# Attention and two MLPs on one core: six half buffers of values for four, block 0's sums allocated later, another order of loads

## The chip, the cores and the metric

The kernel runs on one core of a Trainium2 chip. The metric is the device time of one execution in microseconds (us), the median over several runs. Profiles come from one further execution taken with the hardware profiler; their times count from the span's start.

## The reference

The reference computes attention for 4 batches (blocks below) of 8 heads, with 32 global and 512 local rows of 64 numbers, and sends all 2304 rows of 512 numbers through two MLPs. A local row sees the 32 global keys and the local keys within a distance of 32; a global row sees all 544 keys.

```
mask = np.abs(pos[:, None] - pos[None, :]) <= window      # window = 32
out_g = matmul(softmax(scale * q_g @ k_all^T), v_all)
out_l = matmul(softmax([scale * q_l @ k_g^T, masked scale * q_l @ k_l^T]), [v_g, v_l])
x = concat(out_g, out_l) -> (2304, 512)
h = x @ w_in;  g = where(h > 0, h, exp(min(h, 0)) - 1);  x = g @ w_out        # 512 -> 2048 -> 512
h = x @ w_in2; g = where(h >= 1, h, where(h <= -1, 0, (h + 1)**2 / 4)); y = g @ w_out2
```

## The kernel before

**Two stages.** Lines 634 to 750 are attention, written in a fixed order: every instruction goes through `Pinned` (lines 103 to 111), which keeps each engine's program order, and shows as L111 in the profile. Lines 754 to 820 are the two MLPs; from `eng = free` (line 751) on, the framework's scheduler orders the instructions. Numbers of 32 bits are split into a high and a low part (`xh`, `xl`, `gh`, `gl`, `wh`, `wl`), so that each product is made of three matmuls.

**Attention in slots.** Two heads are a pair: pairs 0 to 15, four to a block. `units` (line 634) holds 24 units in threes: the local rows of an even pair 2g, the global rows of pairs 2g and 2g+1, the local rows of the odd pair 2g+1. The loop at line 719 runs slots n = 0 to 25. In slot n the engines do: scores of unit n (TensorE, tiles `s` or `sg`), division by the sums for unit n-2 (VectorE, `den`, `o_sb`, `og`), transposes of unit n-1 (TensorE `pt` or `tg`, copied by ScalarE to `pT` or `pgT`), transposes of unit n-2 (`ot` or `tg3`, which the trace names `tg`), its high and low part (`xh`, `xl`), the maximum and exponential of unit n (`sn`, `nml`), one step of the weights' preparation, one or two steps of the first five MLP tiles (`early_ups`, from slot 9 on), and the product of unit n-1 with the values (`po` or `pog`). A triple of slots below is slots 3g to 3g+2; s(n) means the scores of slot n.

**What each unit needs.** Scores of a local unit read queries `q_sb` and spread keys `kw`, which GpSimd builds from `k_sb` (`spread_keys`, four instructions for a pair, two for each half). Scores of a global unit read `k_sb` and `diag`, which GpSimd fills from the queries of both its pairs (`spread_queries`). The product with values reads `v_sb`, two half buffers a pair; the global unit reads both halves of both its pairs. There are two buffers each of `q_sb` and `k_sb`, four of `kw` and four half buffers of values (`load_v`, line 415, `bufs=4`).

**Loads.** `load` (line 124) issues on SyncE's queue, in program order. Each load counts the 4-byte words that it brings a partition: 544 for queries, 576 for keys, 1040 for half of a pair's values, 1024 for a part of the weights. From the seventh load on it waits until so many of its elders have landed that at most 2700 words are under way (`IN_FLIGHT`). It also waits, in the queue, until the last reader of its buffer is done. `arrive(n)` (line 700) runs at each slot's end. In slot 3g (g > 0) it sends the odd pair's first half of values, in slot 3g+1 the queries and keys of pair 2g+2 and the odd pair's second half, in slot 3g+2 the queries and keys of pair 2g+3 and both halves of pair 2g+2.

**Weights.** Three tiles of the first MLP's weights are prepared during attention, as six parts of 512 columns. They share one buffer `wraw`. A part is sent at the end of slots 1, 3, 6, 9, 12 and 15 (line 744). Its three steps (lines 178 to 198: VectorE `rest`, then `top`, then `power` and `wl`) run one a slot from slot `PREP_AT = 2` on; the second step is the last reader of `wraw`.

**Storage.** `acc0`, block 0's sums (8 KB a partition), is allocated in `xpool` (line 371) before attention, although its first write comes in slot 24. The tile `e` (2 KB, line 255) of the second MLP's curve is in `t_p`, also open throughout. `zeros` (1 KB, line 642) feeds the ten warm-up matmuls `idle`.

Of the kernel before, what the change touches and what calls it, by code (L numbers as in the profile page):

```python
# [9 lines left out]
F32 = mybir.dt.float32  # L10
BF16 = mybir.dt.bfloat16
# [9 lines left out]
B, H, SL, SG, D = 4, 8, 512, 32, 64  # L21
# [4 lines left out]
P = 128  # L26
NPAIR = H // 2
NSUB = SL // 32
VW = D + 1
KPAD = S + 32  # L30
KT = DM // P
# [15 lines left out]

BANKS = (2, 3, 1)

PREP_AT = 2  # L50
UP_AT = 9

UP_STEP = 4
# [11 lines left out]
def band_attention_then_two_mlps(  # L65
# [21 lines left out]
    xpool = ctx.enter_context(tc.tile_pool(name="x", bufs=1))  # L87
    t_p = ctx.enter_context(tc.tile_pool(name="tmp", bufs=2))
    h_p = ctx.enter_context(tc.tile_pool(name="h", bufs=LAG + 2))
    ps_up = [ctx.enter_context(tc.tile_pool(name="ps_up", bufs=1, space=PSUM))]  # L90
    ps_dn = []

    mask_sb = const.tile([P, 3, P], F32, name="mask_sb")
    eye_sb = const.tile([P, P], F32, name="eye_sb")
# [6 lines left out]
    acc = {}  # L101
# [17 lines left out]
    eng = pinned  # L119
# [4 lines left out]
    def load(out, src, words):  # L124

        ins = eng.sync.dma_start(out, src)
        if eng is not pinned:
            return
        flying, older = words, len(loads)
        while older and flying + loads[older - 1][1] <= IN_FLIGHT:  # L130
            older -= 1
            flying += loads[older][1]
        if older and len(loads) >= FIRST_LOADS:
            tc.add_manual_dep(
                ins.ins, loads[older - 1][0].ins.name, LANDED, reason="loads in flight"
            )
        loads.append((ins, words))
# [6 lines left out]
    for layer in range(2):  # L144
        f = 0
# [4 lines left out]
    def add_ring(pool, i):  # L150

        n = max(len(fs) for _, fs in chunks[i::2])
        ring[i] = [pool.tile([P, n, WCOLS], F32R, name=f"w{nm}{i}") for nm in "hl"]
# [62 lines left out]
    class Up:  # L216
# [31 lines left out]
        def curve(self):  # L248
            self.g = t_p.tile([P, SL], F32, tag="g", name="g")[:, :self.n]
            if self.layer == 0:  # L250
                eng.scalar.activation(self.g, self.ps, AF.Exp)  # L251

                eng.scalar.activation(self.g, self.g, AF.Relu, bias=one_sb, scale=-1.0)  # L253
            else:
                self.e = t_p.tile([P, SL], F32, tag="e", name="e", bufs=1)[:, :self.n]
                eng.scalar.activation(self.g, self.ps, AF.Relu, bias=half_sb, scale=0.5)  # L256
                eng.scalar.activation(self.e, self.ps, AF.Relu, bias=nhalf_sb, scale=0.5)  # L257

# [108 lines left out]
    def mpool(name, bufs, **kw):  # L367
        return ctx.enter_context(tc.tile_pool(name=name, bufs=bufs, reuse_waits="tile", **kw))

    add_ring(ctx.enter_context(tc.tile_pool(name="w", bufs=1)), 0)  # L370
    acc[0] = xpool.tile([P, KT, SL], F32, name="acc0")
    prep_ctx = ExitStack()
    wtmp_p = prep_ctx.enter_context(tc.tile_pool(name="wtmp", bufs=1))

    with ExitStack() as actx:
        def apool(name, bufs, **kw):
            return actx.enter_context(tc.tile_pool(name=name, bufs=bufs, **kw))
# [3 lines left out]
        st_p = apool("st", 4, side="right")  # L381
        sp_p = apool("sp", 4, side="right")
        raw_p = apool("raw", 2, side="right")
        win_p = apool("win", 4, side="right")
        g_p = apool("gl", 1, side="right")
# [4 lines left out]
            tc.tile_pool(name="ps_s", bufs=BANKS[0], space=PSUM, side="right")  # L390
        )

        diag = [g_p.tile([P, 64], F32, name=f"diag{i}") for i in range(4)]

        def normalised(po, out):

# [3 lines left out]
            eng.vector.reciprocal(den, den)  # L400
            eng.vector.tensor_tensor(out, po[..., 0:D], den.to_broadcast([P, *n, D]), ALU.mult)

        loaded = {}
        half = NSUB // 2

        def load_qk(b, hp):
            q_sb = raw_p.tile([P, S], F32, tag="q", name="q_sb")
            k_sb = raw_p.tile([P, KPAD], F32, tag="k", name="k_sb")
            both = [(q_sb, qT), (k_sb, kT)]
            for sb, dram in both if b + hp else both[::-1]:  # L410
                load(sb, dram[b, hp], sb.shape[1])
            loaded[b, hp] = [q_sb, k_sb, diag[(NPAIR * b + hp) % 4], [], []]

        def load_v(b, hp, es=(0, 1)):
            for e in es:
                v_sb = win_p.tile([P, half, 2, VW], F32, tag="v", name="v_sb", bufs=4)
                load(v_sb, vwin[b, hp, :, half * e:half * e + half], half * 2 * VW)
                loaded[b, hp][4].append(v_sb)

        def spread_keys(b, hp):  # L420

            k_sb, kws = loaded[b, hp][1], loaded[b, hp][3]
            for e in range(2):
                kw = win_p.tile([P, half, P], F32, tag="kw", name="kw")
                band = bass.AP(
                    tensor=k_sb.tensor,
                    offset=k_sb.offset + SL // 2 * e,
                    ap=[k_sb.ap[0], [32, half], [1, 96]],
                )
                glob = bass.AP(  # L430
                    tensor=k_sb.tensor, offset=k_sb.offset, ap=[k_sb.ap[0], [0, half], [1, 32]]
                )
                if b + hp + e == 0:
                    eng.vector.tensor_copy(kw[:, :, 0:96], band)
                    eng.scalar.activation(kw[:, :, 96:P], glob, AF.Copy)
                else:
                    eng.gpsimd.tensor_scalar(kw[:, :, 0:96], band, 1.0, 1.0, ALU.mult, ALU.mult)
                    eng.gpsimd.tensor_scalar(kw[:, :, 96:P], glob, 1.0, 1.0, ALU.mult, ALU.mult)
                kws.append(kw)

        def spread_queries(b, hp):

            for c in (hp - 1, hp):
                if hp % 2:
                    q_sb, dq = loaded[b, c][0], loaded[b, c][2]
                    for h in range(2):
                        r = 64 * h
                        eng.gpsimd.tensor_scalar(
                            dq[r:r + 64, 32 * h:32 * h + 32], q_sb[r:r + 64, 0:32], 1.0, 1.0,
                            ALU.mult, ALU.mult,  # L450
                        )
# [186 lines left out]
        pairs = [(b, hp) for b in range(B) for hp in range(NPAIR)]  # L638

        halves = [(f, c0, WCOLS // 2) for c0 in (0, WCOLS // 2) for f in range(W_EARLY)]  # L640

        zeros = st_p.tile([P, 512], BF16, name="zeros", bufs=1)
        eng.vector.memset(zeros, 0.0)
        eng.vector.memset(half_sb, 0.5)
        eng.scalar.activation(st_p.tile([P, 1], F32, name="unused", bufs=1), half_sb, AF.Exp)
        idle = ps_s.tile([P, 512], F32, tag="s", name="idle")
# [4 lines left out]
        eng.scalar.dma_start(eye_sb, eye)  # L651
        load_qk(*pairs[1])
        load_v(*pairs[0])
        for t in diag:
            eng.vector.memset(t, 0.0)
        eng.vector.memset(nhalf_sb, -0.5)
        eng.vector.memset(one_sb, 1.0)
        spread_keys(*pairs[0])
# [6 lines left out]
        def early_weights():  # L665

            for part in parts:
                for _ in range(3):
                    next(part, None)
                    yield  # L670
# [19 lines left out]
        sent = iter(parts)  # L690
        weights, ups = early_weights(), early_ups()
# [8 lines left out]
        def arrive(n):  # L700

            g, r = divmod(n, 3)
            more = 2 * g + 2 < len(pairs)
            if r == 0 and 2 * g + 1 < len(pairs):
                if g:
                    load_v(*pairs[2 * g + 1], es=(0,))
                    spread_queries(*pairs[2 * g + 1])
            elif r == 1 and 2 * g + 1 < len(pairs):
                if more:
                    load_qk(*pairs[2 * g + 2])  # L710
                load_v(*pairs[2 * g + 1], es=(1,) if g else (0, 1))
                spread_keys(*pairs[2 * g + 1])
            elif r == 2 and more:
                load_qk(*pairs[2 * g + 3])
                load_v(*pairs[2 * g + 2])
                spread_keys(*pairs[2 * g + 2])

        live, first = {}, {}
        for n in range(len(units) + 2):
            if n > UP_AT:  # L720
                next(ups, None)
            part(n, "scores")
            part(n - 2, "norm")
            part(n - 1, "turn")
            part(n - 1, "copy")
            part(n - 2, "back")
            part(n - 2, "high")
            part(n, "top")
            part(n - 2, "low")
            part(n, "expo")  # L730
            if n >= PREP_AT:
                next(weights, None)
            if n >= UP_AT:
                next(ups, None)
            part(n - 1, "values")

            arrive(n)
            if n == len(units):

                s_ctx.close()  # L740
                ps_dn.append(mpool("ps_dn0", 1, space=PSUM))
                for f in chunks[0][1]:
                    down(0, chunks[0][1], 0, f, made[0, f, 0], first, range(KT // 2))
            if n == 1 or n % 3 == 0 < n:
                next(next(sent, iter([0])))
        for _ in weights:
            pass
        for _ in ups:
            pass
        prep_ctx.close()  # L750
        eng = free


# [1 line left out]
    for j in range(1, B):  # L755
        acc[j] = pool.tile([P, KT, SL], F32, name=f"acc{j}")
    acc[GR] = pool.tile([P, KT * P], F32, name="acc_rows")
    wraw_p = mpool("wraw", 1, side="right")
    wtmp_p = mpool("wtmp", 1, side="right")
    add_ring(mpool("w_more", 1, side="right"), 1)  # L760
# [124 lines left out]
```

## Time and profile before

| | |
|---|---|
| median of 3 runs | 871.76 us |
| lowest, highest | 871.65, 876.94 us |
| the profiled execution's own time | 871.46 us |
| its span, first to last instruction | 869.7 us |
| TensorE busy | 851.4 us, 98% of the span |
| VectorE, ScalarE, GpSimd busy | 584.3, 432.7, 47.6 us |
| moved by DMA | 65.43 MB |

The profiled execution took 1.76 us more than its span, and lies 0.30 us under the median. Its page divides the span into 40 slices of 21.7 us; the first six are attention. In rows of the time order, the number after a bracket is the idle time of the engine just before the row, and the name behind the arrow is what ended it.

### The profile page before, as it was taken

To read this page: it belongs to the slowest core of one execution; us is meant where nothing else is said; L and a number is where in the kernel's file an instruction comes from. 1 tells how busy PE (TensorE), PEld (TensorE's weight loads), DVE (VectorE), ACT (ScalarE), POOL (GpSimd) and SP (SyncE) were. 2 spreads that over 40 slices of the span, in tenths; PEclk is the share of its full clock that TensorE was granted. 3 is DMA by queue.
4 is the path that set the end of the run, shared out by engine and by line. 5 is a ranking of instruction groups with operands and counts; after the bars stand their busy time and mean duration, and the time that the engine had idled before them with its cause. 6 is when DMAs were issued, how large, how long until landed. Compare 5 with 4: busy or idle time off the path is not lost.

```text
span 869.7 us, 14553 instructions
## 1 busy us (share of the span) xinstructions
PE 851.4 (98%) x5946; PEld 697.9 (80%) x5946; DVE 584.3 (67%) x1130; ACT 432.7 (50%) x755; POOL 47.6 (5%) x98
## 2 busy tenths in 40 slices
PE   7889999999999999999999999999999999999998
PEld 5667778888888888888888888888888888888886
DVE  4769874877636873833389897368859754845455
ACT  5758774766434543534257564456435433433332
POOL 4324320000000000000000000000000000000000
PEclk9989999999999999999999999999999999999999
DMA  7767751231200220110012112002201200000014
GB/s 258 246 220 246 235 176 58 104 131 52 94 1 1 96 97 1 49 48 1 1 49 96 49 50 97 0 4 97 95 0 49 97 1 1 0 1 1 2 58 148
DMA packets 19027, 65.43 MB, mean 75 GB/s; under 512 B 3984, under 2 KB 4240, under 8 KB 15248
## 3 DMA queue, kind: packets, MB, share of 16 engines
q1 hardware_dynamic: 18672, 64.23, 21.3%
q8 instruction: 47, 0.77, 0.3%
q10 hardware_dynamic: 288, 0.26, 0.1%
q14 instruction: 20, 0.16, 0.1%
HBM read 60.03 MB, written 4.46 MB: 74 GB/s over the span
## 4 chain that ended last, share of the span: by engine, by line
PE 91%; DMA 5%; DVE 2%; ACT 1%; issue 0%; SPq 0%
PE dn L318 40%; PE up L245 39%; DMA v_sb<-in_vwin 3%; PE up L242 3%; PE dn L335 3%; DMA wraw<-in_w 2%; PE up L111 1%; PE pt L111 1%; PE s L111 1%; PE po L111 1%; PE pog L111 1%; PE sg L111 1%; PE dn L111 0%; PE tg L111 0%; DVE rest L111 0%; DVE top L111 0%
## 5 line engine op out<-in xcount | busy, mean ns | idle before, releaser
L318 PE MATMUL dn<-gh,wh 128*128 128x512 f32 x506 | 196.9, 389 | 0.0
L318 PE MATMUL dn<-gl,wh 128*128 128x512 f32 x506 | 196.8, 389 | 0.0
L318 PE MATMUL dn<-gh,wl 128*128 128x512 f32 x506 | 196.3, 390 | 0.0
L245 PE MATMUL up<-xh,wl 128*128 128x512 f32 x492 | 192.4, 391 | 0.0
L245 PE MATMUL up<-xl,wh 128*128 128x512 f32 x492 | 191.6, 390 | 0.0
L245 PE MATMUL up<-xh,wh 128*128 128x512 f32 x492 | 191.6, 389 | 0.0
L276 ACT ACTIVATE gh<-g 128x512 fp32r<-128x512 f32 x123 | 77.8, 632 | 118.7 <-DVE g L265 71.9
L295 DVE TENSOR_TENSOR acc<-dn,acc 128x512 f32<-128x512 f32 x128 | 84.9, 686 | 48.5 <-PE dn L318 48.4
L280 DVE TENSOR_TENSOR gl<-g,gh 128x512 fp32r<-128x512 f32 x123 | 84.7, 689 | 39.1 <-ACT gh L276 38.1
L318 PEld LDWEIGHTS dn<-gl,wh 128*128 128x128 f32 x506 | 95.0, 188 | 19.9
L318 PEld LDWEIGHTS dn<-gh,wh 128*128 128x128 f32 x506 | 95.0, 188 | 19.5
L318 PEld LDWEIGHTS dn<-gh,wl 128*128 128x128 f32 x506 | 95.0, 188 | 19.3
L245 PEld LDWEIGHTS up<-xh,wh 128*128 128x128 f32 x492 | 92.3, 188 | 19.3
L245 PEld LDWEIGHTS up<-xl,wh 128*128 128x128 f32 x492 | 92.4, 188 | 18.8
L245 PEld LDWEIGHTS up<-xh,wl 128*128 128x128 f32 x492 | 92.4, 188 | 18.7
L256 ACT ACTIVATE g<-up,half_sb 128x512 f32<-128x512 f32 (+1 forms) x69 | 47.0, 680 | 113.5 <-PE up L245 104.7
L264 DVE SCALAR_TENSOR_TENSOR g<-g 128x512 f32<-128x512 f32 (+1 forms) x69 | 46.9, 680 | 59.4 <-ACT g L256 59.4
L262 DVE SCALAR_TENSOR_TENSOR g<-up,g 128x512 f32<-128x512 f32 x64 | 43.5, 679 | 62.9 <-ACT g L253 62.9
L251 ACT ACTIVATE g<-up 128x512 f32<-128x512 f32 x64 | 37.8, 591 | 87.5 <-PE up L245 82.1
L265 DVE TENSOR_TENSOR g<-g,e 128x512 f32<-128x512 f32 (+1 forms) x69 | 47.0, 681 | 3.6
L178 ACT ACTIVATE top<-wraw 128x1024 f32<-128x1024 f32 x29 | 33.6, 1160 | 27.8 <-DMA wraw<-in_w 24.0
L257 ACT ACTIVATE e<-up,nhalf_sb 128x512 f32<-128x512 f32 (+1 forms) x69 | 46.6, 676 | 0.3 <-DVE g L265 0.3
(112 smaller groups left out, 955.1 us busy)
## 6 DMA issues: line engine op xcount, KB each, us to landing
wraw<-in_w SPq DMA_DIRECT2D x29, 1024.0 KB, 4.8
v_sb<-in_vwin SPq DMA_DIRECT2D x32, 520.0 KB, 4.5
k_sb<-in_kT SPq DMA_DIRECT2D x16, 288.0 KB, 3.8
q_sb<-in_qT SPq DMA_DIRECT2D x16, 272.0 KB, 4.2
outT<-acc SPq DMA_DIRECT2D x16, 256.0 KB, 2.1
wraw<-in_w SPq DMA_DIRECT2D x6, 512.0 KB, 4.7
outT<-acc_rows SPq DMA_DIRECT2D x4, 64.0 KB, 2.2
mask_sb<-in_mask ACTq DMA_DIRECT2D x1, 192.0 KB, 3.3
```

Of the source, the lines that this page charges most:

```text
L111: return lambda *args, **kw: tc.keep_in_program_order(fn(*args, **kw))
L245: eng.tensor.matmul(self.ps, w, x, start=k == 0, stop=k == 3 * KT - 1)
L251: eng.scalar.activation(self.g, self.ps, AF.Exp)
L256: eng.scalar.activation(self.g, self.ps, AF.Relu, bias=half_sb, scale=0.5)
L257: eng.scalar.activation(self.e, self.ps, AF.Relu, bias=nhalf_sb, scale=0.5)
L262: eng.vector.scalar_tensor_tensor(g, self.ps, 0.0, g, ALU.max, ALU.subtract)
L264: eng.vector.scalar_tensor_tensor(g, g, 1.0, g, ALU.min, ALU.mult)
L265: eng.vector.tensor_tensor(g, g, self.e, ALU.add)
L276: eng.scalar.activation(self.gh, self.g, AF.Copy)
L280: eng.vector.tensor_tensor(self.gl, self.g, self.gh.bitcast(F32), ALU.subtract)
L295: eng.vector.tensor_tensor(a, ps, a, ALU.add)
L318: eng.tensor.matmul(banks[d], w[:, d * P:(d + 1) * P], g, start=f == fs[0] and k == 0, stop=f == fs[-1] and k == 2,)
```

## The change

Six half buffers of values stand in place of four. The room comes from `acc0`, now allocated at slot 24 after the preparation's scratch pool is closed, from `e`, allocated after attention in a pool of its own, and from `zeros`, now the same storage as the four `diag` tiles (one memset for both).

`arrive` sends in another order. In slot 0 the values of pair 1; in slot 1 the queries and keys, then the values, of pair 2; in slot 3g (g > 0) both halves of pair 2g+2; in slot 3g+1 its queries and keys; in slot 3g+2 the queries and keys of pair 2g+3, then a part of the weights, then both halves of pair 2g+3. So the parts of the weights are sent in slots 2, 5, 8, 11, 14 and 17, and are prepared from slot 4 on. GpSimd spreads the even pair's keys in slot 3g+1, not 3g+2, and the odd pair's in slot 3g, not 3g+1. No computation is added or removed.

```diff
-PREP_AT = 2
+PREP_AT = 4
...
-                self.e = t_p.tile([P, SL], F32, tag="e", name="e", bufs=1)[:, :self.n]
+                self.e = e_p[0].tile([P, SL], F32, tag="e", name="e")[:, :self.n]
...
-    acc[0] = xpool.tile([P, KT, SL], F32, name="acc0")
...
-        diag = [g_p.tile([P, 64], F32, name=f"diag{i}") for i in range(4)]
+        diags = g_p.tile([P, 4, 64], F32, name="diags")
+        diag = [diags[:, i] for i in range(4)]
...
-                v_sb = win_p.tile([P, half, 2, VW], F32, tag="v", name="v_sb", bufs=4)
+                v_sb = win_p.tile([P, half, 2, VW], F32, tag="v", name="v_sb", bufs=6)
...
-        zeros = st_p.tile([P, 512], BF16, name="zeros", bufs=1)
-        eng.vector.memset(zeros, 0.0)
+        eng.vector.memset(diags, 0.0)
+        zeros = diags.rearrange("p i c -> p (i c)").bitcast(BF16)
...
-        for t in diag:
-            eng.vector.memset(t, 0.0)
...
             g, r = divmod(n, 3)
-            more = 2 * g + 2 < len(pairs)
-            if r == 0 and 2 * g + 1 < len(pairs):
+            even, odd = 2 * g, 2 * g + 1
+            if odd >= len(pairs):
+                return
+            if r == 0:
                 if g:
-                    load_v(*pairs[2 * g + 1], es=(0,))
-                    spread_queries(*pairs[2 * g + 1])
-            elif r == 1 and 2 * g + 1 < len(pairs):
-                if more:
-                    load_qk(*pairs[2 * g + 2])
-                load_v(*pairs[2 * g + 1], es=(1,) if g else (0, 1))
-                spread_keys(*pairs[2 * g + 1])
-            elif r == 2 and more:
-                load_qk(*pairs[2 * g + 3])
-                load_v(*pairs[2 * g + 2])
-                spread_keys(*pairs[2 * g + 2])
+                    spread_queries(*pairs[odd])
+                spread_keys(*pairs[odd])
+                if not g:
+                    load_v(*pairs[odd])
+                elif even + 2 < len(pairs):
+                    load_v(*pairs[even + 2])
+                return
+            if even + 2 < len(pairs):
+                load_qk(*pairs[even + r + 1])
+            if r == 1:
+                if not g:
+                    load_v(*pairs[even + 2])
+                if even + 2 < len(pairs):
+                    spread_keys(*pairs[even + 2])
+            else:
+                next(next(sent, iter([0])))
+                if even + 2 < len(pairs):
+                    load_v(*pairs[even + 3])
...
             if n == len(units):
 
+                for _ in weights:
+                    pass
+                prep_ctx.close()
+                acc[0] = mpool("acc0", 1).tile([P, KT, SL], F32, name="acc0")
...
-            if n == 1 or n % 3 == 0 < n:
-                next(next(sent, iter([0])))
...
+    e_p.append(mpool("e", 1, side="right"))
     wraw_p = mpool("wraw", 1, side="right")
```

## Rows read from the trace of the kernel before

**Rows 1.** The page's 40 slices: granted clock in tenths, GB/s moved by DMA.
```profile
PEclk9989999999999999999999999999999999999999
...
GB/s 258 246 220 246 235 176 58 104 131 52 94 1 1 96 97 1 49 48 1 1 49 96 49 50 97 0 4 97 95 0 49 97 1 1 0 1 1 2 58 148
```
**Rows 2.** Stretches from slot 3 by threes, then the MLPs: busy (x instructions), clock, DMA share, GB/s.
```profile
17.66:34.81 17.15, 12.45 (x329) 9.56 (x327) 13.42 (x56) 11.52 (x30) 6.30 (x11) 1.00 0.80 268
34.81:52.36 17.55, 14.42 (x329) 11.04 (x327) 12.49 (x54) 10.84 (x29) 6.72 (x16) 0.81 0.71 225
52.36:68.89 16.53, 16.48 (x341) 12.84 (x339) 11.97 (x54) 10.71 (x28) 4.72 (x8) 0.89 0.68 225
68.89:85.23 16.34, 14.84 (x340) 11.50 (x339) 14.72 (x57) 13.17 (x35) 6.86 (x14) 1.00 0.74 238
85.23:101.37 16.14, 14.80 (x340) 11.43 (x339) 12.94 (x56) 11.56 (x30) 6.00 (x14) 1.00 0.72 238
101.37:116.64 15.27, 14.82 (x340) 11.43 (x339) 13.29 (x56) 12.46 (x34) 6.06 (x12) 1.00 0.66 219
116.64:130.94 14.30, 14.27 (x340) 11.35 (x339) 9.90 (x50) 11.37 (x32) 3.23 (x6) 1.00 0.46 154
130.94:865.00 734.06, 734.06 (x3347) 609.28 (x3346) 486.25 (x700) 341.19 (x519) 0.00 (x0) 1.00 0.13 47
```
**Rows 3.** Waits of TensorE over the span: us in total, times, longest.
```profile
PE pog L111 <- DMA v_sb<-in_vwin: 6.2, 5, 2.8
PE ot L111 <- DVE o_sb L111: 2.5, 5, 0.9
PE s L111 <- issue: 1.5, 2, 1.3
```
**Rows 4.** TensorE in order of time, slots 2, 3, 5, 8, 9 and 12.
```profile
16.70 1.03 PE L111 MATMUL pog<-v_sb,pgT 64*64 64x130 f32 x10 [0.20 <-DMA v_sb<-in_vwin]
...
21.24 0.34 PE L111 MATMUL tg<-eye_sb,og 128*64 128x64 f32 x4 [1.40 <-DVE og L111]
...
33.85 1.03 PE L111 MATMUL pog<-v_sb,pgT 64*64 64x130 f32 x10 [2.12 <-DMA v_sb<-in_vwin]
...
50.68 1.75 PE L111 MATMUL pog<-v_sb,pgT 64*64 64x130 f32 x10 [2.75 <-DMA v_sb<-in_vwin]
...
54.25 1.97 PE L111 MATMUL pt<-eye_sb,sn 128*128 128x128 f32 x8
...
69.98 1.09 PE L111 MATMUL pt<-eye_sb,sn 128*128 128x128 f32 x8
...
72.39 1.11 PE L111 MATMUL po<-v_sb,pT 128*32 128x65 f32 x64
```
**Rows 5.** Two short stretches, columns as in rows 2.
```profile
36.00:38.00 2.00, 2.00 (x14) 1.57 (x8) 1.78 (x16) 0.60 (x1) 2.00 (x4) 0.50 1.01 368
...
16.70:31.78 15.08, 12.45 (x326) 9.56 (x326) 11.56 (x54) 9.96 (x27) 3.27 (x7) 1.00 0.82 266
```
**Rows 6.** VectorE in order of time, slot 3: the weights' first step.
```profile
19.34 0.43 DVE L111 TENSOR_SCALAR rest<-wraw 128x512 uint32<-128x512 uint32 x1 [3.49 <-DMA wraw<-in_w]
```
**Rows 7.** Waits of SyncE's queue from 26 to 60 us.
```profile
SPq L111 <- DMA v_sb<-in_vwin: 12.5, 6, 3.2
SPq L111 <- PE po L111: 5.2, 2, 3.8
```
**Rows 8.** DMA issues on the page: count, size of one, median us from issue to landing.
```profile
v_sb<-in_vwin SPq DMA_DIRECT2D x32, 520.0 KB, 4.5
k_sb<-in_kT SPq DMA_DIRECT2D x16, 288.0 KB, 3.8
q_sb<-in_qT SPq DMA_DIRECT2D x16, 272.0 KB, 4.2
...
wraw<-in_w SPq DMA_DIRECT2D x6, 512.0 KB, 4.7
```
**Rows 9.** GpSimd in order of time: keys of pair 4 spread.
```profile
31.78 2.96 POOL L111 TENSOR_SCALAR kw<-k_sb 128x768 f32<-128x768 f32 x4 [8.27 <-DMA k_sb<-in_kT]
```

More of the change, by code (lines that the diff above doesn't have):

```diff
@@ L91, in band_attention_then_two_mlps @@
     ps_dn = []
+    e_p = []
     mask_sb = const.tile([P, 3, P], F32, name="mask_sb")
@@ L401, in normalised @@
             eng.vector.tensor_tensor(out, po[..., 0:D], den.to_broadcast([P, *n, D]), ALU.mult)
-        loaded = {}
+        loaded, landed = {}, {}
         half = NSUB // 2
@@ L411, in load_qk @@
                 load(sb, dram[b, hp], sb.shape[1])
-            loaded[b, hp] = [q_sb, k_sb, diag[(NPAIR * b + hp) % 4], [], []]
+            loaded[b, hp] = [q_sb, k_sb, diag[(NPAIR * b + hp) % 4], []]
+            loaded[b, hp].append(landed.setdefault((b, hp), []))
         def load_v(b, hp, es=(0, 1)):
             for e in es:
-                v_sb = win_p.tile([P, half, 2, VW], F32, tag="v", name="v_sb", bufs=4)
+                v_sb = win_p.tile([P, half, 2, VW], F32, tag="v", name="v_sb", bufs=6)
                 load(v_sb, vwin[b, hp, :, half * e:half * e + half], half * 2 * VW)
-                loaded[b, hp][4].append(v_sb)
+                landed.setdefault((b, hp), []).append(v_sb)
         def spread_keys(b, hp):
@@ L743, in band_attention_then_two_mlps @@
                     down(0, chunks[0][1], 0, f, made[0, f, 0], first, range(KT // 2))
-            if n == 1 or n % 3 == 0 < n:
-                next(next(sent, iter([0])))
-        for _ in weights:
-            pass
         for _ in ups:
             pass
-        prep_ctx.close()
         eng = free
```

## The prediction

> **What bounds the kernel now.** I read the page's slices first, then the waits, then attention cut into triples of slots. In the slices the reader sees one dip of TensorE's clock, in the second and third slice, and data at 220 to 258 GB/s up to the fifth and 176 in the sixth [rows 1]. From 130.94 to 865 us TensorE is busy for 734.06 of 734.06 us [rows 2]: the MLPs have no gap that a change of loads could close. So the time is the moment at which attention's last triple ends, 130.94, plus a fixed rest, and only the first 131 us are in play.
>
> There the triples take 17.15, 17.55, 16.53, 16.34, 16.14, 15.27 and 14.30 us, while TensorE works 12.45 in the first (no MLP tile yet) and 14.80 to 14.84 in the fourth to sixth, at full clock [rows 2]. The waits give the reason: the global unit's product waits for the second half of the odd pair's values, 6.2 us over five times, behind it 2.5 us for `o_sb` and 1.5 us of issue [rows 3]. The two long ones are 2.12 us before 33.85 and 2.75 us before 50.68 [rows 4]. After each the granted clock falls: 0.50, which is the level of 1.2 GHz, from 36 to 38 [rows 5], and a mean of 0.81 over the triple from 34.81 [rows 2]. That triple has the same 329 matmuls as the one before and is busy for 14.42 instead of 12.45, so the half clock cost 1.97 us there [rows 2]; one line shows it, eight transposes in 1.97 at 54.25 against 1.09 at 69.98 [rows 4].
>
> Why are values late? SyncE's queue is in order. From 26 to 60 us it waited 12.5 us for older values to land (the rule of 2700 words) and 5.2 us for the product of a local unit to free a buffer [rows 7]. The second kind is what two more buffers can take away. The first kind is a limit of rate: 266 GB/s from 16.70 to 31.78 [rows 5], 225 in the next triple [rows 2].
>
> **The change part by part.** *Bytes.* A triple needs four halves of values, two pairs of queries and keys and a part of weights; by the sizes [rows 8] 4 x 0.532 + 2 x 0.573 + 0.524 = 3.80 MB. Before it took 17.15 us. At 266 GB/s it takes 14.3. That rate is the one I carry on, being the row with the fewest buffer waits; its ends are 250 (between it and the 225 of the next triple) and 300 (a short stretch of 36 to 38 moves 368 [rows 5], which a mean cannot keep, since each load waits for landings).
>
> *The values' wait.* Values are now sent three slots or more ahead of their product, so the 6.2 us go. What is late next is the even pair's keys: for pairs 4, 6, ... they now stand on the queue behind both halves of the pair's own values, and before their scores GpSimd must spread the first half, about half of 2.96 us, 1.5 [rows 9]. Up to pair 2's keys both kernels send the same set of loads; before, the last of it, a half of values, landed at 16.70 [rows 4]. So pair 2's keys land near 16.7 and s(3) starts at 18.2, against 17.66 [rows 2]. From there to pair 4's keys the queue carries values 2, queries and keys 3, a weight part, values 3, values 4, queries and keys 4: 3 x 1.065 + 2 x 0.573 + 0.524 = 4.87 MB, 18.3 us at 266 GB/s. They land at 35.0; s(6) starts at 36.5, 1.7 us later than the 34.81 of before [rows 2]. TensorE's work of 12.45 us ends at 30.7, so one gap of almost 6 us replaces many small ones.
>
> *The clock.* After gaps of 2.12 and 2.75 us the clock fell [rows 4, 5]; I charge 1.97 us for this larger one, between 0 (hidden, as TensorE waits anyway) and twice that, 3.9. The Trainium skill speaks against the change here: its page "TensorE: Matmul & The Clock Gate", section "What's actually happening", says that the array falls to half clock when it has recently been idle; so gathering the waits into one gap would be worse than spreading them. The trace agrees, with the two falls above. By that rule the sum stays at the 868.0 below; without a fall s(9) would be set by the loads' 50.8 us instead of 50.9, and the sum would be 867.9. The last rival below is built on the two falls in the rows alone.
>
> *Up to slot 9.* Loads: pair 6's keys come 3.80 MB after pair 4's, at 35.0 + 14.3 = 49.3, spread by 50.8. TensorE: 36.5 + 12.45 + 1.97 = 50.9. The later one, 50.9, against 52.36 before: 1.5 us won.
>
> *Slots 9 to 23.* From slot 9 on the MLP tiles raise TensorE's work to 14.84 a triple, over the 14.3 of the loads, so TensorE is the bound. I add 0.3 for the waits on `o_sb` that stay, half of what rows 3 divide over eight triples at most (2.5 / 8), and take 15.1 for three triples, with the 1.3 us of issue [rows 3] left where it is: s(18) at 50.9 + 45.3 + 1.3 = 97.5, against 101.37. The sixth triple stays at 15.27: 112.8. The last gets 0.1 to 0.2 more, because the weights' last steps now fall into slots 19 to 21, not 17 to 19: 14.4, so attention's triples end at 127.2, against 130.94. Won: 3.7 us.
>
> *The weights' order.* The first step waited on VectorE for its words until 19.34 [rows 6], and `og` behind it held TensorE for 1.40 us at 21.24 [rows 4]. Sent one slot later but used two slots later, the words have a slot more; the wait should go. It pays for s(3) being later and is inside the 12.45. The second part's wait for the buffer (second step of the first, slot 5) now holds the values behind it on SyncE's queue: between nothing and 3.8 us, the longest buffer wait there [rows 7]. I take nothing, since at 266 GB/s the landing rule holds these loads longer anyway: 9.3 MB must have been sent by then, which takes until after 30 us, when slot 5 ends.
>
> *GpSimd.* Nothing added; it is busy 6.30 of 17.15 us [rows 2], and the queries of the odd pair still go ahead of its keys. Bounds: 0 to the 2.96 of one spreading [rows 9], if an even pair's keys, now first in the queue, arrive late and hold queries behind them. I take 0.
>
> *Storage.* `acc0` is first written in slot 24; the pool that it takes was last read in slot 21. `e` is needed only in the second MLP. `zeros` costs no instruction, and `diag` waits for warm-up matmuls that end before the first keys' scores. All at 0; the cover is that TensorE has other work from 130.94 on [rows 2]. Without it a late first copy would cost at most what one of the waits in rows 3 does, 2.8 us; a gain has no reason, since nothing goes but a few small memsets.
>
> **The sum.** The profiled execution, 871.46 with its span and the 1.76 around it, less 3.7 is 867.8; it lies 0.30 under the median, so I forecast a median of 868.0 us, 0.4% less. A change under 1%, 863.0 to 880.5 here, is about what a measurement of this kernel cannot tell from none.
>
> **Rivals.** *The loads run faster (chance 0.15).* With no buffer waits 300 GB/s: pair 4's keys at 16.7 + 16.2 = 32.9, s(6) at 34.4, pair 6's 12.7 later at 45.6, s(9) at 47.1, TensorE likewise (34.4 + 12.45 = 46.9, clock loss hidden). Then three triples at 14.84, 1.3, 14.82 and 14.27: 122.0, won 8.9, so 862.8. For it: the 368 of one short stretch [rows 5], and 5.2 of 34 us of buffer waits [rows 7]; against: most waits there were for landings.
>
> *Nothing comes of it (0.18).* At 250 GB/s pair 4's keys land at 36.2, s(6) is at 37.7, later triples take 15.2 until s(12) at 68.1, 0.8 before the 68.89 of before; TensorE then takes 15.1 a triple as above and attention ends 1 to 2 us earlier: 870 to 871. This is also the case in which the change does not do what it says: the third pair of buffers fills, but the landing rule, not the buffers, sets the rate.
>
> *Slower (0.12).* The gap before the even pair's scores returns in each triple and drops the clock each time. Then the product of s(3g), which frees the buffers for the next values, ends late, and the chain closes on itself: 4.6 us from scores to the product's end (s(12) at 68.89 [rows 2], product from 72.39 for 1.11 [rows 4]), 1.97 for half clock, 4.5 for values to land, 3.8 for keys behind them [rows 8], 1.5 to spread them [rows 9]: 16.4 a triple. From 36.5 on, six of them end at 134.9, 4.0 later than now: 875.8. It decides from the point at which this chain exceeds TensorE's 15.1; without the clock's 1.97 it is 14.4 and loses.
>
> **How the numbers follow.** Forecast 0.50, with a range of its own of 865 to 870.5; the rivals as given; 0.05 for what I do not see. The range 862.8 to 876 leaves out half of the first rival and half of the last, and little else. Faster by over 1% is the better half of the first rival and a tail: 0.10. Slower by over 1% needs the chain above with more than one clock drop a triple: 0.04. Within: 0.86.
>
> **What would show it.** Right: no wait of `pog` on `v_sb` over 1 us; GpSimd waits for keys in slots 4 and 7, and s(6) starts at 35 to 38 behind an idle TensorE; clock 0.5 just after; from slot 9 on triples of 15 us; no wait of `rest` for `wraw`; a stretch of the MLPs as long as before, 734 us. Wrong: s(6) before 33 (loads much faster), a triple after slot 9 over 16 us, low clock behind slot 12, or idle TensorE behind attention's end.

## The result and the profile after

The changed kernel takes 882.68 us (882.12 to 884.53), the kernel before 873.02 us (870.49 to 876.94, six runs beside it): a ratio of 1.011 with an interval of 1.0088 to 1.0131. The forecast was 868.0 with a range up to 876, so it failed in sign and in range. The profiled execution took 883.01 us with a span of 881.2, against 869.7 before: 11.5 us more.

Lines moved by one, so L112 of the changed kernel answers to L111. First the page's slices, clock and GB/s:

```profile
PEclk9899999999999999999999999999999999999999
...
GB/s 254 205 216 247 216 221 51 96 96 69 114 9 1 63 117 12 48 49 1 1 48 52 92 49 96 0 1 96 96 0 49 96 1 0 1 1 1 1 53 151
```

Against [rows 1], the second and third slice fell from 246 and 220 to 205 and 216 GB/s, and the sixth rose from 176 to 221: the same bytes, later. The stretches from s(3), s(6), ... s(21), and the MLPs, columns as in [rows 2] (stretch, length, busy of TensorE, weight load, VectorE, ScalarE, GpSimd, clock, DMA share, GB/s):

```profile
18.55:41.34 22.79, 14.18 (x327) 10.79 (x327) 10.97 (x52) 10.36 (x28) 5.54 (x13) 0.81 0.67 215
41.34:57.77 16.43, 14.07 (x326) 10.71 (x326) 10.40 (x49) 9.36 (x26) 5.58 (x13) 0.85 0.73 236
57.77:75.84 18.07, 14.48 (x340) 11.26 (x338) 15.48 (x61) 13.69 (x37) 6.43 (x13) 1.00 0.67 219
75.84:92.24 16.40, 15.87 (x339) 12.33 (x339) 11.10 (x50) 10.70 (x28) 6.35 (x14) 0.90 0.69 219
92.24:110.33 18.09, 14.48 (x341) 11.44 (x339) 15.63 (x63) 14.21 (x38) 5.51 (x12) 1.00 0.71 228
110.33:127.80 17.47, 16.11 (x339) 12.33 (x339) 11.10 (x50) 10.69 (x28) 7.04 (x16) 0.90 0.66 216
127.80:142.49 14.69, 14.32 (x340) 11.35 (x338) 12.06 (x54) 11.87 (x33) 3.05 (x6) 1.00 0.25 78
142.49:876.50 734.01, 734.01 (x3347) 609.25 (x3346) 486.35 (x700) 340.54 (x519) 0.00 (x0) 1.00 0.13 47
```

The last row is the one of before to 0.05 us: the MLPs and the moved storage cost nothing. The whole loss lies ahead of 142.49, which was 130.94 in [rows 2]: 11.55 us. Half of it, 5.64 us, is in the first triple (22.79 against 17.15); of the later ones three are over 17 us.

TensorE's waits over the span name what took the place of the wait for values:

```profile
PE s L112 <- POOL kw L112: 16.9, 8, 7.8
PE s L112 <- issue: 3.8, 4, 2.0
...
PE pog L112 <- DMA v_sb<-in_vwin: 0.2, 1, 0.2
```

The 6.2 us for values and the 2.5 us for `o_sb` [rows 3] are down to 0.2 each. In their place local scores wait 16.9 us for spread keys. In order of time TensorE shows where (start, length, and in brackets the idle time ahead):

```profile
18.55 0.83 PE L112 MATMUL s<-kw,q_sb 64*32 64x128 f32 x32 [1.28 <-POOL kw L112]
19.71 1.11 PE L112 MATMUL s<-kw,q_sb 64*32 64x128 f32 x32 [0.33 <-POOL kw L112]
...
32.55 1.03 PE L112 MATMUL pog<-v_sb,pgT 64*64 64x130 f32 x10 [0.17 <-DMA v_sb<-in_vwin]
41.34 2.27 PE L112 MATMUL s<-kw,q_sb 64*32 64x128 f32 x64 [7.76 <-POOL kw L112]
...
75.84 0.67 PE L112 MATMUL s<-kw,q_sb 64*32 64x128 f32 x32 [2.78 <-POOL kw L112]
...
110.33 0.67 PE L112 MATMUL s<-kw,q_sb 64*32 64x128 f32 x32 [2.98 <-POOL kw L112]
```

These are s(3), the product of slot 5, s(6), s(12) and s(18): each long wait for keys is ahead of an even pair's scores. GpSimd was free and waited for the keys of pair 4 themselves; it began to spread them at 40.08:

```profile
40.08 2.36 POOL L112 TENSOR_SCALAR kw<-k_sb 128x768 f32<-128x768 f32 x4 [13.44 <-DMA k_sb<-in_kT]
```

Why so late? SyncE's queue in order of time, its waits from 24 to 32 us, and its waits for VectorE over attention (us in total, times, longest):

```profile
22.69 0.33 SPq L112 DMA_DIRECT2D wraw<-in_w  x1
23.41 0.33 SPq L112 DMA_DIRECT2D v_sb<-in_vwin  x1
...
28.27 1.59 SPq L112 DMA_DIRECT2D v_sb<-in_vwin  x2
...
32.57 0.33 SPq L112 DMA_DIRECT2D v_sb<-in_vwin  x1
...
34.27 0.33 SPq L112 DMA_DIRECT2D k_sb<-in_kT  x1
```
```profile
SPq L112 <- DMA wraw<-in_w: 4.5, 1, 4.5
...
SPq L112 <- DVE top L112: 6.7, 2, 3.9
```

From 24 to 32 us the queue waited for no buffer (its other wait there was 0.9 us for older values), yet it issued nothing from 23.8 to 28.2. With the weight part (1024 words) and a half of values (1040) under way, a third large load would make 3104 words, over 2700, so it stood until the weights had landed. The traffic shows the hole, and a second one at 58, where the queue waited for VectorE's second step of the weights (`top`) with values behind it:

```profile
28.00:30.00 2.00, 1.95 (x69) 1.56 (x70) 1.90 (x6) 0.93 (x2) 0.00 (x0) 1.00 0.37 81
...
58.00:60.00 2.00, 1.22 (x66) 0.75 (x51) 1.91 (x4) 1.02 (x4) 1.92 (x4) 1.00 0.02 9
```

Three causes suggest themselves: **the place in line** of the keys (behind both halves of their own pair's values), **the fit of the landing rule** (a weight part and four halves of values in a row, of which only two go at a time), and **the weights' hold** on the queue. The experiments take them one by one, and the last runs together. Each ratio below is to the kernel before, run on the same chip beside it. The first four runs (up to the buffers alone), the next four (up to keys first with the larger window) and the last three stand on three chips, so a difference "by medians" between these groups is rougher than a ratio. The waits and stretches of each run come from its one profiled execution; with the larger window in the changed kernel, the small loads and the weights alone it took 2.3 to 3.0 us less than the median.

### The profile page after: what moved, and what is told of

It is laid out like the page before. It is cut to its first block, busy times and chain, and to the rows that moved or that the text cites. A ratio compares the mean times of both kernels' runs of the same rounds, so it can differ in the third digit from the quotient of the medians.

```text
span 881.2 us, 14554 instructions
## 1 busy us (share of the span) xinstructions
PE 852.4 (97%) x5946; PEld 698.5 (79%) x5946; DVE 582.8 (66%) x1126; ACT 431.3 (49%) x755; POOL 45.7 (5%) x98
## 4 chain that ended last, share of the span: by engine, by line
PE 93%; DMA 3%; POOL 1%; DVE 1%; ACT 1%; issue 0%; POOLq 0%; SPq 0%
PE dn L319 39%; PE up L246 38%; PE up L243 3%; PE dn L336 2%; DMA k_sb<-in_kT 2%; PE pt L112 2%; PE po L112 2%; PE up L112 2%; PE s L112 2%; POOL kw L112 1%; PE sg L112 1%; DMA v_sb<-in_vwin 1%; PE tg L112 1%; PE idle L112 0%; PE dn L112 0%; PE ot L112 0%
## 5 line engine op out<-in xcount | busy, mean ns | idle before, releaser
L246 PEld LDWEIGHTS up<-xh,wh 128*128 128x128 f32 x492 | 92.3, 188 | 19.3
L254 ACT ACTIVATE g<-g,one_sb 128x512 f32<-128x512 f32 x64 | 45.9, 717 | 1.8
```

Source lines behind the costliest of these rows:

```text
L246: eng.tensor.matmul(self.ps, w, x, start=k == 0, stop=k == 3 * KT - 1)
```

## The experiments

**A larger window.**
```diff
-IN_FLIGHT = 2700
+IN_FLIGHT = 3200
```
First in the changed kernel:

> The changed kernel, with one number altered: 3200 words may be under way in place of 2700, so that three large loads (3 x 1040 = 3120) fit at once. Theory A, the landing rule: in the new order five large loads stand in a row (a weight part, four halves of values), of 2700 words only two of them fit, so the loads move 215 GB/s from s(3) to s(6) where the order before moved 268. Then this run moves 250 GB/s or more there, s(6) starts at 36 to 38 us in place of 41.3, and the time is 872 to 877 us. Rival B, the place in line: the even pair's keys are late only because 1.07 MB of values stand ahead of them; the rate is what the chip gives this mix. Then s(6) stays at 40 to 42 us and the time within 2 us of the changed kernel's 882.7.

Measured: 875.01 us, ratio 1.0038 (1.0008 to 1.0068). Its first triple, TensorE's waits and two of the queue's waits:

```profile
18.58:34.06 15.48, 11.84 (x328) 9.30 (x326) 11.97 (x55) 11.31 (x33) 6.04 (x13) 1.00 0.87 289
```
```profile
PE s L112 <- POOL kw L112: 6.3, 9, 1.9
```
```profile
SPq L112 <- DVE top L112: 17.9, 5, 4.0
SPq L112 <- PE s L112: 17.8, 8, 4.5
```

289 GB/s in place of 215, s(6) at 34.06 in place of 41.34 (earlier than A's 36 to 38), the wait for keys down from 16.9 to 6.3 us: A holds for the rate, B falls. So 215 GB/s was not the most that this mix of loads could get. But the time stays above before, and the queue now waits for the weights' second step and for scores, so the window is not the whole of it. What it leaves lies late: from s(9) to s(21) the four triples still took 67.13 us, where by the rows above the changed kernel took 70.03 and by [rows 2] the kernel before 64.28:

```profile
50.34:117.47 67.13, 60.08 (x1354) 46.19 (x1352) 54.90 (x222) 49.43 (x129) 27.16 (x52) 0.97 0.69 230
```

The control, the same number in the kernel before:

> The kernel before, with 3200 words under way in place of 2700; the control of the run above. If the larger window is worth the same in any order, this gains as much as the run above does. Theory A expects less here, since before no more than three large loads stand in a row and two buffers pairs hold them back anyway: 0 to 3 us faster than before (870 to 873). Rival B: no difference.

Measured: 872.43 us, ratio 0.9994 (0.9971 to 1.0018). Its queue's longest wait in total:

```profile
SPq L111 <- PE po L111: 25.3, 7, 5.7
```

No difference: with four half buffers the words that the window lets go have nowhere to land (at 2700 words this wait, for the local product to free a buffer, was 10.7 us). With the storage and order of before, the larger window is worth nothing that can be measured.

**The keys ahead of the pair's values.** Order alone, 2700 words.
```diff
                 if not g:
                     load_v(*pairs[odd])
-                elif even + 2 < len(pairs):
-                    load_v(*pairs[even + 2])
                 return
...
             if r == 1:
-                if not g:
-                    load_v(*pairs[even + 2])
                 if even + 2 < len(pairs):
+                    load_v(*pairs[even + 2])
                     spread_keys(*pairs[even + 2])
```

> The changed kernel, but the even pair's queries and keys go ahead of that pair's values: both are sent in slot 3g+1, none in slot 3g. Theory A and B both expect s(6) earlier by the 1.07 MB of values that no longer stand ahead, about 5 us at 215 GB/s: 36 to 37 us. B expects that this mends the whole loss: no wait of the scores for keys over 1 us and 868 to 873 us. A expects the rate from s(3) to s(6) to rise as well, since the row of five large loads is broken into two: 240 GB/s or more.

Measured: 869.81 us, ratio 0.9956 (0.9936 to 0.9976). The first triple and the waits for keys:

```profile
21.24:35.69 14.45, 13.18 (x326) 10.39 (x326) 9.49 (x47) 8.92 (x25) 6.43 (x14) 0.88 0.81 266
```
```profile
PE s L112 <- POOL kw L112: 5.3, 3, 3.1
```

s(6) at 35.69, and the rate up to 266. This one move mends the whole loss and 3 us more. It changes two things, the keys' place and the row of five large loads (now three and two), so by itself it doesn't tell them apart; the run of keys first and the larger window together does. B's "no wait over 1 us" was too much: the longest, 3.1 us, is ahead of s(3). Up to there this kernel sends the same loads in the same order as the changed one, where s(3) came at 18.55 and not at 21.24, so that difference is between executions. The four triples from s(9), which the window had left long, are now as short as before:

```profile
50.62:114.39 63.77, 59.84 (x1352) 46.53 (x1352) 53.77 (x221) 48.25 (x124) 26.21 (x52) 0.97 0.79 256
```

**The buffers alone.** The storage of the change; loads, spreading and weights as before.
```diff
-PREP_AT = 4
+PREP_AT = 2
```
(and `arrive` and the place of `sent` as in the kernel before)

> The storage of the changed kernel (six half buffers of values, block 0's sums, e and zeros moved) with the order of loads, spreading and weights of the kernel before. Theory: the loss lies in the order alone, and the buffers only take away waits of the queue for a freed buffer (5.2 us between 26 and 60 us before): 866 to 871 us, no slower than before. Rival: storage itself costs (a late first copy into the sums, or idle TensorE after attention): 876 us or more, with gaps behind attention's end.

Measured: 871.53 us, ratio 0.9978 (0.9958 to 0.9999). The old wait is all there:

```profile
PE pog L112 <- DMA v_sb<-in_vwin: 6.8, 5, 2.5
```

So the storage costs nothing, and in the old order six buffers bring 1 to 2 us at most (0.9 by medians, and the interval all but touches 1): values are sent in the slots in which they were sent before. The loss is in the order of loads, spreading and weights.

**Small loads.** Does the larger window help by its size or by its fit?
```diff
-FIRST_LOADS = 6
+FIRST_LOADS = 8
...
-                load(v_sb, vwin[b, hp, :, half * e:half * e + half], half * 2 * VW)
+                for i in range(0, half, half // 2):
+                    a = half * e + i
+                    load(v_sb[:, i:i + half // 2], vwin[b, hp, :, a:a + half // 2], half * VW)
```

> The changed kernel with its 2700 words and its order of loads, but each half of values is sent as two loads of 520 words in place of one of 1040 (and the first eight loads, not six, go without a wait, so that the same bytes do). Theory A, the landing rule fits coarse loads badly: five small loads (2600 words) fit where two large ones (2080) did, so the stretch from s(3) to s(6) moves 250 GB/s or more in place of 215, and the time is 873 to 877, as with the larger window. Rival C: the larger window helped by its sheer size (more words under way), not by its fit; then this run moves at most 230 GB/s there and stays at 880 or more.

Measured: 876.45 us, ratio 1.0038 (1.0016 to 1.0061). Its first two triples:

```profile
17.55:34.20 16.65, 11.86 (x326) 9.40 (x326) 11.42 (x53) 10.75 (x31) 5.53 (x13) 0.95 0.87 283
34.20:52.05 17.85, 14.52 (x327) 11.09 (x327) 10.49 (x49) 9.48 (x26) 7.03 (x16) 0.86 0.67 214
```

283 GB/s with the same 2700 words: the fit, not the size of the window (five loads of 520 words go at a time where two of 1040 did). It gains about what 500 more words do. The second triple, 17.85 us, shows what the fit doesn't mend.

**The weights' place.** In the changed kernel, behind the odd pair's values:
```diff
             else:
-                next(next(sent, iter([0])))
                 if even + 2 < len(pairs):
                     load_v(*pairs[even + 3])
+                next(next(sent, iter([0])))
```

> The changed kernel, but the part of the weights is sent behind the odd pair's values, not ahead of them. Theory D: the weights' wait for their buffer (the second step on VectorE, 6.7 us of the queue's time in the changed kernel) holds the values and the keys behind it; behind the values it still stands ahead of the next even pair's keys, so the keys are hardly earlier: 879 to 884 us, the scores' wait for keys within 4 us of the 16.9 of the changed kernel. Rival E: that the weights go ahead of the values is what costs: 876 us or less.

Measured: 878.29 us, ratio 1.0063 (1.0041 to 1.0085), between the two forecasts.

```profile
PE s L112 <- POOL kw L112: 9.9, 8, 3.6
```

7.0 us less of waiting for keys than in the changed kernel: D, which allowed 4, falls, and so does E's 876. The weights' place is a part of the loss, some 4 us of it, and not the largest. Its triples from s(3), s(9) and s(15):

```profile
19.55:38.98 19.43, 13.30 (x326) 10.30 (x326) 11.02 (x52) 10.48 (x29) 5.56 (x13) 0.88 0.76 251
...
56.14:72.76 16.62, 16.11 (x338) 12.41 (x339) 10.53 (x49) 10.81 (x28) 6.31 (x14) 0.90 0.63 220
...
87.87:103.90 16.03, 15.05 (x340) 11.44 (x338) 14.37 (x58) 12.88 (x35) 6.66 (x13) 1.00 0.76 243
```

The queue no longer waits for `top` at all. The two triples in which such a wait ended in the changed kernel are 1.45 and 2.06 us shorter, but the first triple, in which the queue had not waited for `top`, is 3.36 us shorter too. So the hold by `top` is at most a part of what this move gives back.

In the kernel before, the weights alone as changed:
```diff
-PREP_AT = 2
+PREP_AT = 4
...
-            elif r == 2 and more:
-                load_qk(*pairs[2 * g + 3])
-                load_v(*pairs[2 * g + 2])
-                spread_keys(*pairs[2 * g + 2])
+            elif r == 2:
+                if more:
+                    load_qk(*pairs[2 * g + 3])
+                if 2 * g + 1 < len(pairs):
+                    next(next(sent, iter([0])))
+                if more:
+                    load_v(*pairs[2 * g + 2])
+                    spread_keys(*pairs[2 * g + 2])
...
-            if n == 1 or n % 3 == 0 < n:
-                next(next(sent, iter([0])))
```

> The kernel before (four half buffers, its order of values and keys), with only the weights as changed: sent in slots 2, 5, 8 and so on ahead of the even pair's values, prepared from slot 4 on. Theory: the first step no longer waits for its words (1.40 us of TensorE in slot 3), and little else: 870 to 873 us. Rival E: the weights' new place ahead of values costs: 876 us or more, with more waits of the global product for values.

Measured: 873.14 us, ratio 0.9997 (0.997 to 1.0023).

```profile
PE pog L111 <- DMA v_sb<-in_vwin: 4.6, 4, 2.0
PE s L111 <- issue: 3.1, 3, 1.9
```

No cost there, and no gain, although the queue waited 13.6 us for `top` in this run. The weights' place does no harm in the old order with four half buffers; that it costs in the new one because of the row of values around it is the likely reading, not one that a run shows by itself.

**Keys first and the larger window together.**

> Keys ahead of the even pair's values, and 3200 words under way. If place in line and fit of the window are two separate losses, both gains add up in part: 865 to 869 us. If the keys' place alone had been the limit of that kernel, it stays at 869 to 871, as with 2700 words.

Measured: 865.90 us, ratio 0.9924 (0.9897 to 0.9951), the lowest median of the study, 16.8 us under the changed kernel. TensorE does not wait for values and waits 0.5 us for keys, once; its largest wait in total, the first two triples, and the four from s(9) to s(21):

```profile
PE s L112 <- issue: 5.4, 5, 2.4
```
```profile
18.37:31.30 12.93, 12.04 (x328) 9.38 (x327) 9.76 (x50) 10.18 (x30) 6.62 (x14) 1.00 0.92 319
31.30:48.55 17.25, 14.14 (x328) 11.05 (x326) 13.33 (x56) 11.19 (x32) 7.36 (x16) 0.90 0.76 251
...
48.55:110.98 62.43, 58.18 (x1354) 45.61 (x1352) 52.05 (x222) 48.72 (x127) 24.77 (x48) 1.00 0.75 247
```

The first triple runs at 12.93, which is TensorE's own work of 12.04 and little else; not all are so good (17.25 from s(6)). This run tells place and fit apart. With 3200 words in both, moving the keys takes the time from 875.01 to 865.90, 9.1 us by medians: the keys' place costs even where three large loads fit, and the four triples from s(9) fall from 67.13 to 62.43. With the keys first in both, the window takes it from 869.81 to 865.90, 3.9 us. In the changed order the window had given 7.7 and the keys' place 12.9, so the two gains add only in part (16.8 together, not 20.5), and the place is the larger. Three variations around it:

> Six half buffers and their storage, the order of loads of the kernel before, and 3200 words under way. If the buffers are of use only where the window lets more loads go, this gains over the buffers alone (871.5 at 2700 words): 866 to 869 us. If the order (keys of the even pair two slots ahead, values later) is what the gain of the keys-first kernel rests on, it stays at 870 to 873.

Measured (old order, six buffers, 3200): 869.78 us, ratio 0.9956 (0.9929 to 0.9983). It fell between the two forecasts, 1.8 us under the buffers alone by medians. The intervals of the two overlap, so that the window is worth something in the old order with six buffers is likely, not shown; nor is it shown that the 3 us from here to keys first with the same window (0.9956 to 0.9924) are more than noise, as the intervals overlap there too.

```profile
PE po L112 <- issue: 5.7, 2, 3.4
```

> Keys first, 3200 words, and the weights behind the odd pair's values. In the kernel with 3200 words the queue still waits 19.3 us for VectorE's second step of the weights, with values behind it. If that wait still reaches TensorE, this gains 1 us or more on 865.9; if it is hidden by the lead of the values, the time is the same within 1 us.

Measured: 868.62 us, ratio 0.9951 (0.9922 to 0.998), with runs from 863.49 to 872.04. No gain; weights ahead of the values are not worse once the keys go first. The spread is too wide to call it a loss. The queue's wait for `top` went from 19.3 us in the kernel with keys first and 3200 words to 1.8 here (its wait for scores rose from 9.8 to 24.5), so taking this hold away brought nothing that can be measured there:

```profile
SPq L112 <- DVE top L112: 19.3, 5, 4.6
```
```profile
SPq L112 <- DVE top L112: 1.8, 2, 1.1
```

> Keys first with 4300 words under way in place of 3200 (four large loads). TensorE's waits in the kernel with 3200 are nearly all issue (5.4 us), none for keys or values, so a larger window has nothing left to give: 865 to 868 us. Rival: more words under way hold the instructions' own fetches up longer, and issue waits grow: 868 us or more.

Measured: 866.78 us, ratio 0.9935 (0.9908 to 0.9962): nothing left to give, as expected.

```profile
PE s L112 <- issue: 6.1, 4, 3.5
```

## Why the prediction was wrong

**Right: what goes and what is late next.** Values' waits went (6.2 to 0.2 us), the weights' first step no longer waits, the even pair's keys became the bound with TensorE idle ahead of s(6) and half clock behind it, and the MLPs took 734.01 us. s(3) was forecast at 18.2 and came at 18.55; with the same loads up to there it came at 21.24 with the keys first and at 19.55 with the weights behind the values, so the near hit is partly luck.

**The step that failed first: the rate carried on.** "They land at 35.0" rested on 266 GB/s, taken from a stretch of the old order as the row "with the fewest buffer waits". GpSimd could begin on them at 40.08 only. Counted from 17.30, when it began on pair 2's keys, 4.87 MB took 22.8 us: 214 GB/s (the row of the triple has 215), below even the 250 that was my lower end. The rate was a result of the order under the rule of 2700 words, not a property of the queue: with the same order it is 289 with 3200 words, and 283 with small loads. I had written down the rule of 2700 words and the words of each load, and never added up which loads fit together in the new order. That addition (1024 + 1040 + 1040 = 3104) would have shown it. But the rate is only the first part: attention ended 15.3 us later than the forecast 127.2, and of these 4.8 lie up to s(6), 2.0 in the next triple and 8.4 behind s(9).

**The second: "I take nothing" for the weights' hold.** The queue waited 6.7 us in two pieces for VectorE's `top`. The argument was that the landing rule held these loads longer anyway; once the loads are late that isn't so: at 58 us the traffic stood at 9 GB/s for two microseconds. Moving the weights was worth 4.4 us in the changed kernel. How much of that is the hold is open: the largest single gain, 3.36 us, is in a triple without it, and with keys first and 3200 words, taking away 17.5 us of such waits brought nothing.

**The third: "TensorE is the bound from slot 9 on", 15.1 us a triple.** Measured: 18.07, 16.40, 18.09 and 17.47 (the last was forecast at 15.27). The keys were late again ahead of s(12) and s(18), and the clock fell behind each: TensorE's busy time in the triples after these gaps is 15.87 and 16.11 against 14.48. This step failed by itself, not only through the first. With 3200 words the rate was above the 266 that I carried on and s(9) came at 50.34, before the forecast 50.9; still the four triples to s(21) took 67.13 us, where the sum has 61.9 (45.3 + 1.3 + 15.27), and the time was 875.01. With the keys ahead of the values and the same 3200 words they took 62.43. So setting the 14.3 us of a triple's loads against TensorE's work was the wrong test: what counted behind s(9) was the keys' place in line, behind values that were needed later. (The 0.3 us a triple for `o_sb` is all of 2.5 / 8, not half of it; that wait was 0.2 us in all, so the slip changes nothing here.) Why it is every second triple isn't settled; the queue's two waits for `top`, 3.9 and 2.8 us, end in just the two triples of 18 us.

**The slower rival came nearest, in part by luck.** It put 16.4 us on each triple, by a chain from the scores through the freed buffer and the keys back to the scores, and one fall of the clock in each. From s(6) to attention's end six triples took 101.15 us, 16.9 each. Keys that come late again and again are what it foresaw. Its chain isn't what the rows show: the mean clock is below 1.00 in three of the six triples, and over attention the queue waited 5.1 us, twice, for the local product to free a buffer, against 48.2 us for older values and 20.1 for weights to land:

```profile
SPq L112 <- DMA v_sb<-in_vwin: 48.2, 26, 5.0
SPq L112 <- DMA wraw<-in_w: 20.1, 6, 4.5
...
SPq L112 <- PE po L112: 5.1, 2, 2.7
```

Its end, 875.8, was short by s(6) being 4.8 us later than its 36.5 (the rate again), and by 0.5 us a triple. It held 0.12 of the chance; I had put the rate's ends too close together, by rows of another order.

**What stays open.** The clock's own share in the loss wasn't taken apart: no run kept TensorE busy in the gaps. How much of the 10 us belongs to each cause can't be read off as a sum either, since they overlap: fit alone gives back 6 to 8, the weights' place 4.4, the keys' place all 10 and more, and that last one breaks up the row of large loads as well. With 3200 words, where that row matters less, the keys' place still gives back 9.1.

## What to carry to other kernels

A load sent earlier pushes back whatever stands behind it on the same queue; when transfers are the bound, order them by when each is needed, counting the work between landing and use (here GpSimd's spreading), and don't put a prefetch with slots to spare ahead of a load that is needed next. If loads are limited by an amount under way, add up which loads fit together in the new order: a limit a little under three large loads works as a limit of two. More buffers alone were worth 1 to 2 us at most, a larger window alone nothing; with the order mended as well they were worth 7.

## What was not expected of the hardware

The clock fell after a smaller gap than in [rows 4]: in the changed kernel TensorE idled 1.28 us ahead of s(3), then 0.33 within it, and from 20 to 22 us the granted clock was 0.50 (1.2 GHz). In the kernel before, 1.40 us of idle ahead of 21.24 [rows 4] left the mean clock of its triple at 1.00 [rows 2]:

```profile
20.00:22.00 2.00, 2.00 (x38) 1.62 (x23) 1.09 (x11) 0.10 (x1) 0.13 (x1) 0.50 0.96 354
```

And TensorE's waits put down to issue, 1.5 us for scores before [rows 3], are 3.8 in the changed kernel, 5.4 with keys first and 3200 words, and 6.1 with 4300: in these kernels they are longer where more loads may be under way. It isn't a rule: with 3200 words they are 4.2 in the old order with four half buffers and 1.3 with six, where 5.7 us ahead of the local product are put down to issue instead. What TensorE waits for there the profile doesn't say, and no run tested it.
